# First dense layer as a seven-product scheme on pairs of token tiles, with w_out centred beforehand and the layer norm's factor moved to the output

## Chip, cores and metric

One core of one Trainium2 chip runs the whole program. The metric is the device time of a run in microseconds (us).

## What is computed

```python
x = attention(q, k, v)                     # 9 chunks of 64 positions, each for itself
P = exp(logits - max); 8 rounds of row and column scaling
out += P[:, e:e+1] * (relu(x @ w1[e]) @ w2[e])          # 8 experts
h = x @ w_in                               # 2304 x 512 by 512 x 1024: the first dense layer
solu = h * softmax(h)
ln = (solu - mean) / sqrt(var + 1e-6) * g_ln
return ln @ w_out                          # 1024 x 512: the second dense layer
```

w_in and w_out come as 64-bit floats.

## The kernel before

Every product runs on TensorE as three passes: an operand is split into a rounded part and a rest (`split`: ScalarE writes the rounded part, VectorE or GpSimd the rest), and hi\*hi, hi\*lo and lo\*hi are summed in PSUM.

The experts are worked off in 96 units `n` of 7 steps `i`. In step `i`, `l1` makes one of seven products (Winograd's form of Strassen's scheme, `PRODUCTS`: banks X, Y and Z, with VectorE's sums between them), and `l2s` makes a piece of the second expert product of an earlier pair of units; each is 6 matmuls of 384 columns. From unit 32 on both operands are loaded from DRAM through SP's queue (`w_load`, line 621), in the order in which the code issues them; an instruction that waits on a queue holds what is behind it. GpSimd makes `hT` and `ho_T` (`h_sums`, lines 681 and 673), the sums that `l2s` reads from its fourth operand on. `events` is a table of such work by step number. `second_sums` builds ten units' w2 operands on GpSimd and stores them (line 556).

`prep` is a queue of small steps that turn the 64-bit weights into split 32-bit ones (`mlp_steps`): from unit 35 on, one is taken in each of the steps 1, 3 and 5 of a unit. One tile of 128 x 512 takes seven VectorE instructions (lines 921 to 947), then `parts` (the split, GpSimd) and `store` (two DMAs, line 957).

The dense layers stand at the end. For each of 18 token tiles `t`: `mlp_x` loads x, `mlp_a` splits it, `mlp_b` makes h in two banks (24 matmuls of 512 columns, line 1005), the maximum (line 1019) and exp (line 1020); `mlp_n` makes solu (`un`, line 1025), its statistics (line 1030) and the normalised tile (line 1038); `mlp_c` transposes that (line 1050) and splits it; `mlp_d` makes the second product (24 matmuls, line 1062), and ScalarE and a DMA bring it out. The loop runs `mlp_b(s)`, `mlp_c(s - 1)`, `mlp_n(s)`, `mlp_d(s - 2)`. Before it stands the change-over: the 14 last pieces of `l2s` (k = 0 to 13), each in a bank of its own, with `mlp_b(0)` after k = 7.

Of the kernel before, what the change touches and what calls it, by code (L numbers as in the profile page):

```python
# [44 lines left out]
def chunk_attention_sinkhorn_moe_solu_kernel(  # L45
# [865 lines left out]

    def mlp_steps(n):
        i, j = divmod(n, 8)
        s = {}
        ts, stt = nc.vector.tensor_scalar, nc.vector.scalar_tensor_tensor


        def one():
            s["lo"], s["hi"] = raw64[n][:, :, 0], raw64[n][:, :, 1]
            s["b"] = two([P, 512], U32, f"wb{n}")  # L920
# [30 lines left out]
        def parts():  # L951
            s["p"] = [two([P, 512], F32R, f"wp{n}_{s_}") for s_ in range(2)]
            split(*s["p"], s["b"].bitcast(F32), nc.gpsimd)

        def store():
            for s_ in range(2):
                nc.sync.dma_start(
                    out=kept[i, s_][:, j * 512:(j + 1) * 512], in_=s["p"][s_].bitcast(F32)
                )

        return [one, two_, three, round_, rounded, size, flush_, parts, store]
# [3 lines left out]
    def load_in(kk, s_):  # L965
        t = six([P, F], F32R, f"mi{kk}_{s_}")
        nc.sync.dma_start(out=t.bitcast(F32), in_=kept[0, s_][:, kk * F:(kk + 1) * F])
        m_in[kk, s_] = t

    def load_out(n0, n1):  # L970
        for n in range(n0, n1):
            f, s_ = divmod(n, 2)
            if n % 3 == 0:
                m_out["t"] = six([P, 3, DM], F32R, f"mo{n}")
            t = m_out["t"]
            nc.sync.dma_start(
                out=t[:, n % 3].bitcast(F32), in_=kept[1, s_][:, f * DM:(f + 1) * DM]
            )
            m_out[f, s_] = t[:, n % 3]
# [14 lines left out]
    def mlp_a(t):  # L994
        x = xa.pop(t)
        xm[t] = [wtile([P, KD, P], F32R, f"xm{t}_{i}") for i in range(2)]
        split(xm[t][0], xm[t][1], x)

    def mlp_b(t):
        x = xm.pop(t)  # L1000
        ph = bank2(f"mh{t}")
        for n in range(2):
            for kk in range(KD):
                for i, (a, c) in enumerate(PASSES3):
                    nc.tensor.matmul(  # L1005
                        ph[:, n * 512:(n + 1) * 512],
                        x[a][:, kk, :],
                        m_in[kk, c][:, n * 512:(n + 1) * 512],
                        start=(kk == 0 and i == 0),
                        stop=(kk == KD - 1 and i == 2),  # L1010
                    )
# [3 lines left out]
        su = small.tile([P, 1], F32, tag="su", name=f"su{t}")  # L1015
        st = small.tile([P, 2, 6], F32, tag="st", name=f"st{t}")
        mv = small.tile([P, 2], F32, tag="mv", name=f"mv{t}")
        r2 = small.tile([P, 1], F32, tag="r2", name=f"r2{t}")
        nc.vector.tensor_reduce(out=nm, in_=ph, axis=AX.X, op=ALU.max, negate=True)  # L1019
        nc.scalar.activation(out=ex, in_=ph, func=AF.Exp, bias=nm, scale=1.0, accum_out=su)  # L1020
        stage[t] = (ph, ex, un, su, st, mv, r2)

    def mlp_n(t):
        ph, ex, un, su, st, mv, r2 = stage.pop(t)
        nc.vector.tensor_tensor(out=un, in0=ph, in1=ex, op=ALU.mult)  # L1025
# [3 lines left out]
        for i in range(2):  # L1029
# [26 lines left out]
    def mlp_d(t, f0=0, f1=KF):  # L1056
# [15 lines left out]
        nc.scalar.activation(out=ob, in_=po.pop(t), func=AF.Copy)  # L1072
# [3 lines left out]
    with tc.manual_schedule():  # L1076
# [103 lines left out]
        )  # L1180

# [5 lines left out]
        for n, u in enumerate(PLAIN):  # L1187
# [16 lines left out]
        for n in range(NM):  # L1204
# [30 lines left out]
            if n == NM - 1:  # L1235
                for t in range(3):
                    mlp_x(t)
            apart = n < 4
            parts = [(j, d, i) for d in (0, 2) for j in range(2) for i in range(2)]
            for i in range(7):  # L1240
# [9 lines left out]
                if n == NM - 1:  # L1250
                    load_in(*divmod(i, 2))
# [4 lines left out]
                if n > NU + 2 and i in (1, 3, 5) and prep:  # L1256
# [85 lines left out]
```

## Time and profile before

| | |
|---|---|
| median of 3 runs | 1758.02 us (1757.84 to 1758.71) |
| profiled execution | 1758.82 us, its span 1757.0 us |
| PE busy | 1736.6 us (99%), 10809 matmuls |
| DVE (VectorE) busy | 1371.0 us (78%) |
| POOL (GpSimd) busy | 1095.3 us (62%) |
| ACT (ScalarE) busy | 620.0 us (35%) |
| DMA, mean over the span | 274 GB/s |

Spans of time are counted from the first instruction. PE is TensorE's matmul row; busy shares are averages over stages with different limits.

### The profile page before, as it was taken

How to read it: one execution, taken by the hardware profiler on the slowest of the kernel's cores; microseconds unless marked ns; L12 is line 12 of the kernel's file. 1: busy time of each engine (PE TensorE's matmuls, PEld its weight loads, DVE VectorE, ACT ScalarE, POOL GpSimd, SP SyncE). 2: the span in 40 equal slices, each digit the busy share in tenths (PEclk: the TensorE clock that was granted, in tenths of full speed). 3: DMA queues.
4: the chain of work that ended last, by engine and by line, in shares of the span. 5: the costliest groups of instructions: out<-in, count | busy, mean ns of one | idle time of the engine just before them, and what ended most of it. 6: DMA issues, size and time to landing. Idle time of an engine off the chain costs nothing. (4 is left out here: it accounts for less than half of the span.)

```text
span 1757.0 us, 32067 instructions
## 1 busy us (share of the span) xinstructions
PE 1736.6 (99%) x10809; PEld 1683.5 (96%) x10809; DVE 1371.0 (78%) x2258; ACT 620.0 (35%) x1415; POOL 1095.3 (62%) x1203
## 2 busy tenths in 40 slices
PE   8999999999999999999999999999999999999999
PEld 7899999999999999999999999999999999988887
DVE  7878888888987777777777788878787877776664
ACT  6734444444444223333332222222323232223222
POOL 3867889888898277778777756665656565400000
PEclk9999999999999999999999999999999999999999
DMA  9867899899899999989989999888888887921210
GB/s 215 228 218 264 309 317 344 311 336 331 319 324 322 356 329 344 333 296 349 314 293 345 355 337 353 310 285 286 283 265 268 285 273 254 319 99 46 66 49 30
DMA packets 299203, 481.45 MB, mean 274 GB/s; under 512 B 47248, under 2 KB 99616, under 8 KB 299040
## 3 DMA queue, kind: packets, MB, share of 16 engines
q1 hardware_dynamic: 298320, 475.47, 79.2%
q10 hardware_dynamic: 720, 3.93, 0.5%
q8 instruction: 87, 1.43, 0.3%
q14 instruction: 76, 0.62, 0.1%
HBM read 332.94 MB, written 146.35 MB: 273 GB/s over the span
## 5 line engine op out<-in xcount | busy, mean ns | idle before, releaser
L673 POOL TENSOR_TENSOR ho_T<-hT,ho_T 128x384 fp32r<-128x384 f32 x252 | 275.8, 1096 | 195.0 <-ACT ho_T L672 174.7
L796 PE MATMUL y<-h,w_A 128*128 128x384 f32 x1536 | 303.7, 335 | 0.5 <-DVE acc L823 0.5
L796 PEld LDWEIGHTS y<-h,w_A 128*128 128x128 f32 x1536 | 269.1, 188 | 1.4 <-ACT w_S L599 1.1
L672 ACT ACTIVATE ho_B<-hp 128x384 fp32r<-128x384 f32 x192 | 101.0, 526 | 414.7 <-DVE hp L706 406.5
L847 PE MATMUL y<-ho_T,wl_S 128*128 128x384 f32 x1152 | 230.6, 335 | 1.5 <-DMA wl_S<-wk 1.5
L152 POOL TENSOR_TENSOR w_A<-raw,w_A 128x256 fp32r<-128x256 f32 x224 | 173.2, 786 | 82.1 <-ACT w_A L151 77.7
L867 DVE TENSOR_TENSOR acc<-y,acc 128x768 f32<-128x768 f32 (+1 forms) x217 | 199.9, 923 | 23.3 <-PE y L847 23.2
L751 DVE TENSOR_TENSOR t<-Y,s 128x384 f32<-128x384 f32 x192 | 106.2, 553 | 136.6 <-PE Y L653 94.0
L847 PEld LDWEIGHTS y<-ho_T,wl_S 128*128 128x128 f32 x1152 | 202.1, 188 | 3.0 <-issue 1.9
L681 POOL TENSOR_TENSOR hT<-hp,hp 128x384 f32<-128x384 f32 x126 | 133.7, 1083 | 96.5 <-DVE hp L706 86.7
L672 ACT ACTIVATE ho_T<-hT 128x384 fp32r<-128x384 f32 x256 | 131.7, 516 | 124.5 <-POOL hT L681 119.8
L653 PE MATMUL Y<-x_T,wl_S 128*128 128x384 f32 x768 | 154.0, 334 | 0.3 <-DVE t L751 0.3
L847 PE MATMUL y<-ho_B,wl_A 128*128 128x384 f32 x768 | 153.5, 334 | 0.5 <-DMA wl_A<-wk 0.5
L653 PE MATMUL X<-x_B,wl_A 128*128 128x384 f32 x768 | 153.7, 334 | 0.0
L673 DVE TENSOR_TENSOR ho_B<-hp,ho_B 128x384 fp32r<-128x384 f32 x192 | 143.6, 748 | 3.9 <-ACT ho_B L672 3.3
L681 POOL TENSOR_TENSOR hT<-hp,hT 128x384 f32<-128x384 f32 x126 | 144.9, 1150 | 0.0
L1036 POOL TENSOR_TENSOR r<-r,mhalf 128x1 f32<-128x1 f32 x18 | 9.9, 550 | 208.5 <-DVE r L1033 208.5
L847 PEld LDWEIGHTS y<-ho_B,wl_A 128*128 128x128 f32 x768 | 134.8, 188 | 1.0 <-DVE acc L867 0.8
L653 PEld LDWEIGHTS Y<-x_T,wl_S 128*128 128x128 f32 x768 | 134.8, 188 | 0.9 <-DVE t L751 0.9
L653 PEld LDWEIGHTS X<-x_B,wl_A 128*128 128x128 f32 x768 | 135.0, 188 | 0.0
L823 DVE TENSOR_TENSOR acc<-y,acc 128x768 f32<-128x768 f32 (+1 forms) x132 | 118.9, 901 | 5.3 <-PE y L796 4.7
L152 POOL TENSOR_TENSOR w_S<-ws,w_S 128x256 fp32r<-128x256 f32 x128 | 103.0, 822 | 7.8 <-ACT w_S L151 7.8
(169 smaller groups left out, 3453.5 us busy)
## 6 DMA issues: line engine op xcount, KB each, us to landing
wl_S<-wk SPq DMA_DIRECT2D x512, 256.0 KB, 4.9
wl_A<-wk SPq DMA_DIRECT2D x384, 256.0 KB, 4.9
wk<-w_S SPq DMA_DIRECT2D x256, 256.0 KB, 3.6
wk<-w_A SPq DMA_DIRECT2D x192, 256.0 KB, 3.4
raw<-in_moe_w_dram SPq DMA_DIRECT2D x71, 512.0 KB, 6.1
sh<-spread SPq DMA_DIRECT2D x64, 192.0 KB, 5.3
kept<-wp SPq DMA_DIRECT2D x32, 256.0 KB, 4.6
xk_T<-x_T SPq DMA_DIRECT2D x8, 768.0 KB, 4.3
```

What stands on the lines that cost most here:

```text
L152: (eng or nc.vector).tensor_tensor(out=lo, in0=src, in1=hi.bitcast(F32), op=ALU.subtract)
L653: nc.tensor.matmul(b, w[:, a, kk, :], x[:, c, kk, :], start=(first and kk == 0 and n == 0), stop=(kk == 1 and n == 2), skip_group_check=no ...
L672: nc.scalar.activation(out=hi, in_=x, func=AF.Copy)
L673: f = lambda: eng.tensor_tensor(out=lo, in0=x, in1=hi.bitcast(F32), op=ALU.subtract)
L681: eng.tensor_tensor(out=hb[m, n], in0=hb[m, a], in1=hb[m, b], op=ALU.subtract)
L751: nc.vector.tensor_tensor(out=c_of[n], in0=bank_, in1=c_of[other], op=ALU.add)
L796: nc.tensor.matmul(y, wo2[u, f"A{d // 2 + 1}{f + 1}"][:, a, i * P:(i + 1) * P], h[:, c, f, :], start=(f == 0 and n == 0), stop=(f == 1 and ...
L823: nc.vector.tensor_tensor(out=at, in0=y, in1=at, op=ALU.add)
L847: nc.tensor.matmul(y, wo2[unit(m + q_)[1], wn][:, a, i * P:(i + 1) * P], hop[m // 2, bn][:, q_, c, :], start=(q_ == 0 and o == 0), stop=(q ...
L867: nc.vector.tensor_tensor(out=at, in0=y, in1=at, op=ALU.add)
L1036: nc.gpsimd.tensor_tensor(out=r2, in0=r2, in1=mhalf, op=ALU.pow)
```

## The change

- `mlp_b` takes two tiles: A is 256 tokens x 512, B is w_in, each in 2 x 2 blocks. Seven products of 6 matmuls take the place of eight (48 matmuls). `mlp_s` makes the four sums of A's blocks and `mlp_a` splits them, both with GpSimd. B's four sums are made while w_in is converted (`less`), so `store` writes 28 pieces of 256 KB where it wrote 16, and `load_in` fetches them in the order of use. X and C12 lie in the pair's first double bank, C21 and C22 in its second; Y and Z have a single bank each.
- w_out's rows are scaled by g_ln and stored (`put_g`), then `mean_steps` loads them again, adds them up on GpSimd, takes the mean over the 1024 rows with one matmul (`wmean`), subtracts it from each piece, and splits and stores it. So the layer norm needs no mean taken off. Its factor is applied as ScalarE's scale when the output leaves PSUM; `mlp_n` loses two VectorE instructions and gains one of GpSimd.
- `prep` is taken in steps 0, 1 and 2, and in steps 0 to 5 once 64 or fewer are left. The w_in tiles go in the order B11, B12, B22, B21 of each half.
- `second_sums`' last three steps come 1, 3 and 5 steps later; the last pair's w2 loads come 4 steps sooner.
- The loop runs over 9 pairs; the change-over makes a whole pair after k = 7.

```diff
     def mlp_steps(n):
...
+        def store(n_=None):
             for s_ in range(2):
+                k = 4 * M_OPS.index(n_) + 2 * s_ + c
+                to = kept_in[:, k * 512:(k + 1) * 512]
+                nc.sync.dma_start(out=to, in_=s["p"][s_].bitcast(F32))
...
+        put = lambda v: [lambda: parts(v), lambda: store(v)]
+        if name == "B11":
+            return steps[:-1] + [lambda: (flush_(), keep_b())] + put("B11")
+        if name == "B12":
+            return steps[:-1] + [
+                lambda: (flush_(), keep_b()), lambda: less("T1", "B12", "B11")
+            ] + put("T1")
+        if name == "B22":
+            return steps + put("B22") + [
+                lambda: (less("T3", "B22", "B12"), less("T2", "B22", "T1"))
+            ] + put("T3") + put("T2")
+        return steps + put("B21") + [lambda: less("T4", "B21", "T2")] + put("T4")
+
+    def mean_steps():
...
+        r = [lambda: (load(0, vtile), load(1, two), nc.gpsimd.memset(ratio, 1.0 / F))]
+        for j in range(1, 8):
+            r.append(lambda j=j: (load(j + 1, two) if j < 7 else None, add(j)))
+        r += [lambda: None] * 3 + [lambda: (mean(), load(0, two))]
+        for j in range(8):
+            r.append(lambda j=j: (load(j + 1, two) if j < 7 else None, less(j)))
+            r.append(lambda j=j: parts(j))
+            r.append(lambda j=j: store(j))
+        return r
...
+    def mlp_s(r):
+
+        x0, x1 = xa[2 * r], xa[2 * r + 1]
+        ts = nc.gpsimd.tensor_tensor
...
+    def mlp_a(r):
...
+            split(*p, src, nc.gpsimd)
...
+    def mlp_b(r, i):
+
+        wn, xn, bn = PRODUCTS[i]
+        first = i in (0, 1, 4)
...
+        if i == 0:
+            mb["s1"] = two([P, 512], F32, f"ms{r}")
+            nc.scalar.activation(out=mb["s1"], in_=b, func=AF.Copy)
+        for to, x, other in {
+            1: (("t0", b, "s1"),), 3: (("t1", b, "s1"), (r1[:, 512:], mb.get("Z"), "t1")),
+            5: ((r1[:, :512], b, "s1"),), 6: ((r0[:, 512:], b, "t0"),),
+        }.get(i, ()):
...
+            nc.vector.tensor_tensor(out=to, in0=x, in1=mb[other], op=ALU.add)
+        if i == 5:
+            mlp_e(2 * r + 1, r1)
+        elif i == 6:
+            mlp_e(2 * r, r0)
...
-        nc.vector.tensor_tensor(out=r2, in0=r2, in1=su, op=ALU.mult)
-        nc.vector.tensor_scalar(
-            out=un, in0=un, scalar1=mv[:, 0:1], scalar2=r2, op0=ALU.subtract, op1=ALU.mult
-        )
-        ln[t] = un
+        nc.gpsimd.tensor_tensor(out=r2, in0=r2, in1=su, op=ALU.mult)
...
-        nc.scalar.activation(out=ob, in_=po.pop(t), func=AF.Copy)
+        nc.scalar.activation(out=ob, in_=po.pop(t), func=AF.Copy, scale=r2s.pop(t))
...
-                event(g + 7 + k, f[k])
+                event(g + 7 + k + (0, 1, 3, 5)[max(k - 6, 0)], f[k])
...
-                        event(7 * (m + 2) + 2 * n - 5,
+                        event(7 * (m + 2) + 2 * n - (9 if m == NM - 2 else 5),
...
-                if n > NU + 2 and i in (1, 3, 5) and prep:
+                if n > NU + 2 and (i < 3 or len(prep) <= fast and i != 6) and prep:
...
             if k == 7:
-                mlp_b(0)
-                mlp_a(2)
+                for i in M_ORDER:
+                    if i == 5:
+                        mlp_a(1)
+                    mlp_b(0, i)
+                mlp_m(1)
+                mlp_m(0)
...
+        for r in range(1, NR):
+            t1, t0 = 2 * r + 1, 2 * r
+            if r + 1 < NR:
+                mlp_s(r + 1)
+            for i in M_ORDER:
+                mlp_b(r, i)
+                if r == 1 and i == 3:
+                    mlp_n(1)
+                    mlp_n(0)
+            mlp_m(t1)
+            mlp_m(t0)
+            if r + 1 < NR:
+                mlp_a(r + 1)
+            mlp_d(t1 - 2)
+            mlp_c(t1)
+            mlp_n(t1)
+            for _ in range(2):
+                if sums:
+                    sums.popleft()()
...
+            mlp_n(t0)
+            mlp_d(t0 - 2)
+            mlp_c(t0)
```

`M_ORDER` is (0, 1, 4, 3, 2, 5, 6). Three places of the instruction order follow.

VectorE, in the loop of the dense layers. Before, one tile (`lnt`: the split's rest; `un`: solu; `xm`: x):

```order
L1019 TENSOR_REDUCE nm_20577<-mh_20550 128x1
L152 TENSOR_TENSOR lnt_0_1_20585<-lt_0_20588,lnt_0_0_20584 128x512
L152 TENSOR_TENSOR lnt_1_1_20587<-lt_1_20595,lnt_1_0_20586 128x512
L1025 TENSOR_TENSOR un_20576<-mh_20550,ex_20575 128x1024
L1026 TENSOR_SCALAR su_20578<-su_20578 128x1
L1027 RECIPROCAL su_20578<-su_20578 128x1
L1028 TENSOR_TENSOR r_20581<-su_20578 128x1
L1030 BN_STATS st_20579<-un_20576 128x6 x2
L1031 BN_AGGR mv_20580<-st_20579 128x2
L1033 TENSOR_SCALAR r_20581<-mv_20580,r_20581 128x1
L1037 TENSOR_TENSOR r_20581<-r_20581,su_20578 128x1
L1038 TENSOR_SCALAR un_20576<-un_20576,mv_20580,r_20581 128x1024
```

Now, from the second tile's split of one pair into the next pair (`mt`: t0 and t1; `mh`: the two double banks):

```order
L1198 TENSOR_SCALAR r_20428<-mv_20427,r_20428 128x1
L152 TENSOR_TENSOR lnt_0_1_20467<-lt_0_20470,lnt_0_0_20466 128x512
L152 TENSOR_TENSOR lnt_1_1_20469<-lt_1_20477,lnt_1_0_20468 128x512
L1164 TENSOR_TENSOR mt_20507<-mY_20500,ms_20498 128x512
L1164 TENSOR_TENSOR mt_20522<-mY_20500,ms_20498 128x512
L1164 TENSOR_TENSOR mh_1_20491<-mZ_20509,mt_20522 128x512
L1164 TENSOR_TENSOR mh_1_20491<-mY_20500,ms_20498 128x512
L1175 TENSOR_REDUCE nm_20540<-mh_1_20491 128x1
L1164 TENSOR_TENSOR mh_0_20490<-mZ_20509,mt_20507 128x512
L1175 TENSOR_REDUCE nm_20553<-mh_0_20490 128x1
L1181 TENSOR_TENSOR un_20539<-mh_1_20491,ex_20538 128x1024
L1181 TENSOR_TENSOR un_20552<-mh_0_20490,ex_20551 128x1024
```

The first sum of a pair (`mt`, t0) stands behind the statistics and both splits of the tile before it, and the statistics no longer stand ahead of the transposes of their own tile.

GpSimd, two units near the experts' end, before (`hT`, `ho_T`: the second expert product's sums and their splits):

```order
L681 TENSOR_TENSOR hT_18033<-hp_11_17959,hp_01_18003 128x384
L681 TENSOR_TENSOR hT_18035<-hp_01_18003,hp_00_17910 128x384
L673 TENSOR_TENSOR ho_T_18055<-hT_18033,ho_T_18055 128x384
L681 TENSOR_TENSOR hT_18058<-hp_11_17959,hT_18035 128x384
L673 TENSOR_TENSOR ho_T_18100<-hT_18035,ho_T_18100 128x384
L681 TENSOR_TENSOR hT_18103<-hp_10_17980,hT_18058 128x384
L673 TENSOR_TENSOR ho_T_18145<-hT_18058,ho_T_18145 128x384
L673 TENSOR_TENSOR ho_T_18197<-hT_18103,ho_T_18197 128x384
```

And now (`wg`: a scaled piece of w_out, `wp`: its split's rest):

```order
L681 TENSOR_TENSOR hT_18443<-hp_11_18360,hp_01_18409 128x384
L681 TENSOR_TENSOR hT_18445<-hp_01_18409,hp_00_18304 128x384
L673 TENSOR_TENSOR ho_T_18467<-hT_18443,ho_T_18467 128x384
L681 TENSOR_TENSOR hT_18470<-hp_11_18360,hT_18445 128x384
L1031 TENSOR_TENSOR wg_18387<-wg_18387,wmean 128x512
L152 TENSOR_TENSOR wp_1_18516<-wg_18387,wp_0_18515 128x512
L673 TENSOR_TENSOR ho_T_18519<-hT_18445,ho_T_18519 128x384
L681 TENSOR_TENSOR hT_18522<-hp_10_18383,hT_18470 128x384
L1031 TENSOR_TENSOR wg_18490<-wg_18490,wmean 128x512
L673 TENSOR_TENSOR ho_T_18569<-hT_18470,ho_T_18569 128x384
L152 TENSOR_TENSOR wp_1_18618<-wg_18490,wp_0_18617 128x512
L673 TENSOR_TENSOR ho_T_18621<-hT_18522,ho_T_18621 128x384
```

Four instructions of 512 columns now stand among the eight of 384 that `l2s` needs.

SP's queue in the last unit, before (`mi`: w_in's pieces, `wl_..._1`: w2 operands of the last pairs):

```order
L967 DMA mi_0_19018<-kept_0_133 128x1024
L621 DMA wl_A_1_19020<-wk_123 128x512
L621 DMA wl_A_1_19022<-wk_124 128x512
L967 DMA mi_1_19044<-kept_1_134 128x1024
L967 DMA mi_0_19067<-kept_0_133 128x1024
L621 DMA wl_A_1_19069<-wk_125 128x512
L621 DMA wl_A_1_19071<-wk_126 128x512
```

And now:

```order
L621 DMA wl_A_1_19087<-wk_125 128x512
L621 DMA wl_A_1_19089<-wk_126 128x512
L1063 DMA mi_19115<-kept_in 128x512
L1063 DMA mi_19117<-kept_in 128x512
L1063 DMA mi_19119<-kept_in 128x512
L1063 DMA mi_19130<-kept_in 128x1536
L621 DMA wl_A_1_19132<-wk_123 128x512
L621 DMA wl_A_1_19134<-wk_124 128x512
L621 DMA wl_A_1_19140<-wk_125 128x512
L621 DMA wl_A_1_19142<-wk_126 128x512
```

The last pair's first w2 operands (wk_125, wk_126) stand ahead of w_in's pieces instead of between them.

## Rows read from the trace of the kernel before

**Rows 1.** windows; stretch, length, busy us (instructions), clock, DMA share, GB/s

```profile
634.00:1100.00 466.00, 462.02 (x2653) 458.97 (x2652) 367.74 (x562) 139.58 (x301) 346.49 (x341) 1.00 0.94 330
...
1407.00:1506.00 99.00, 99.00 (x573) 99.00 (x572) 69.19 (x105) 27.24 (x57) 59.96 (x59) 1.00 0.82 263
...
1523.00:1559.00 36.00, 34.06 (x172) 29.23 (x171) 26.07 (x52) 7.52 (x15) 3.12 (x4) 1.00 0.65 233
...
1559.00:1754.00 195.00, 194.42 (x923) 161.87 (x921) 122.50 (x233) 53.99 (x98) 8.80 (x16) 1.00 0.15 49
```

**Rows 2.** chain that ended last, dense layers; start, us, what

```profile
1515.81 1.04 PE y L847 x6
...
1700.78 5.49 PE po L1062 x24
...
1706.26 5.44 PE mh L1005 x24
...
1711.71 0.88 PE lt L1050 x8
...
1753.46 0.60 ACT ob L1072
```

**Rows 3.** waits of PE, whole span; total us, times, longest us

```profile
PE Z L653 <- DVE X L751: 2.0, 3, 0.9
...
PE y L847 <- DMA wl_A<-wk: 1.7, 2, 1.2
...
PE y L847 <- DMA wl_S<-wk: 1.5, 2, 1.3
```

**Rows 4.** PE's timeline, change-over; start, us, instructions

```profile
1522.93 4.33 PE L847 MATMUL y<-ho_B,wl_A 128*128 128x384 f32 x24
...
1559.07 5.71 PE L1062 MATMUL po<-mo,lnt 128*128 128x512 f32 x24
```

**Rows 5.** instruction groups from 1560 on; busy us, mean ns, idle before

```profile
L152 DVE TENSOR_TENSOR lnt<-lt,lnt 128x512 fp32r<-128x512 f32 x34 | 21.9, 686 | 31.3 <-ACT lnt L151 31.3
...
L1030 DVE BATCH_NORM_STATS2 st<-un 128x6 f32<-128x512 f32 x32 | 20.5, 683 | 0.0
...
L1019 DVE TENSOR_REDUCE nm<-mh 128x1 f32<-128x1024 f32 x16 | 19.6, 1225 | 21.9 <-PE mh L1005 21.9
...
L1025 DVE TENSOR_TENSOR un<-mh,ex 128x1024 f32<-128x1024 f32 x16 | 19.4, 1215 | 0.0
...
L1020 ACT ACTIVATE ex<-mh,nm 128x1024 f32<-128x1024 f32 x16 | 17.9, 1117 | 92.0 <-DVE nm L1019 92.0
...
L1038 DVE TENSOR_SCALAR un<-un,mv,r 128x1024 f32<-128x1024 f32 x16 | 13.0, 813 | 0.6
...
L875 DVE TENSOR_TENSOR acc<-acc,acc 128x768 f32<-128x768 f32 x7 | 6.7, 953 | 0.0
...
L1033 DVE TENSOR_SCALAR r<-mv,r 128x1 f32<-128x1 f32 x16 | 3.4, 214 | 0.6
```

**Rows 6.** instruction groups of DVE, 634 to 1500

```profile
L751 DVE TENSOR_TENSOR t<-Y,s 128x384 f32<-128x384 f32 x118 | 65.3, 553 | 99.0 <-PE Y L653 59.6 <-POOL hT L681 12.9 <-POOL ho_T L673 10.9
...
L875 DVE TENSOR_TENSOR acc<-acc,acc 128x768 f32<-128x768 f32 x7 | 8.1, 1162 | 0.0
```

**Rows 7.** windows, 5 us of the change-over

```profile
1525.00:1530.00 5.00, 4.42 (x24) 3.78 (x24) 5.00 (x11) 1.52 (x3) 0.15 (x1) 1.00 1.06 386
```

**Rows 8.** DVE's timeline near 740

```profile
738.48 1.50 DVE L925 SCALAR_TENSOR_TENSOR wb<-wd,wb 128x512 uint32<-128x512 uint32 x1
```

**Rows 9.** PE's timeline near 741

```profile
741.37 1.33 PE L653 MATMUL Z<-x_B,wl_S 128*128 128x384 f32 x6 [0.72 <-DVE X L751]
```

**Rows 10.** waits of SP's queue, 634 to 1420

```profile
SPq L556 <- POOL w_S L602: 29.1, 19, 3.0
...
SPq L957 <- POOL wp L152: 13.5, 6, 4.3
```

**Rows 11.** instruction group of POOL, 634 to 1500

```profile
L152 POOL TENSOR_TENSOR wp<-wb,wp 128x512 fp32r<-128x512 f32 x16 | 20.9, 1305 | 17.1 <-ACT wp L151 17.0
```

More of the change, by code (lines that the diff above doesn't have):

```diff
@@ L949, in flush_, with put_g, parts @@
                 nc.scalar.activation(out=f, in_=f, func=AF.Copy, scale=g_sb[:, j:j + 1])
-        def parts():
+        def put_g():
+            nc.sync.dma_start(
+                out=kept_g[:, j * 512:(j + 1) * 512], in_=s["b"].bitcast(F32)
+            )
+        def parts(n_=None):
+            f = s["b"].bitcast(F32) if n_ in (None, name) else carried[n_]
             s["p"] = [two([P, 512], F32R, f"wp{n}_{s_}") for s_ in range(2)]
-            split(*s["p"], s["b"].bitcast(F32), nc.gpsimd)
@@ new lines, in mlp_steps, with keep_b @@
+        steps = [one, two_, three, round_, rounded, size, flush_]
+        if i == 1:
+            return steps + [put_g]
+        def keep_b():
+            carried[name] = s["b"].bitcast(F32)
+        put = lambda v: [lambda: parts(v), lambda: store(v)]
[5 more added lines that the diff above has]
+            ] + put("T1")
@@ new lines, in mlp_steps, with load, add, mean @@
+        if name == "B22":
[4 more added lines that the diff above has]
+    def mean_steps():
+        s = {}
+        def load(j, new):
+            s[j] = new([P, 512], F32, f"wg{j}")
+            nc.sync.dma_start(out=s[j], in_=kept_g[:, j * 512:(j + 1) * 512])
+        def add(j):
+            x = s.pop(j)
+            nc.gpsimd.tensor_tensor(out=s[0], in0=s[0], in1=x, op=ALU.add)
+        def mean():
+            pm = bank("wmean")
+            nc.tensor.matmul(pm, ratio, s.pop(0), start=True, stop=True)
+            s["m"] = vtile([P, 512], F32, "wmean")
+            nc.scalar.activation(out=s["m"], in_=pm, func=AF.Copy)
+        def less(j):
+            nc.gpsimd.tensor_tensor(out=s[j], in0=s[j], in1=s["m"], op=ALU.subtract)
+        def parts(j):
+            s["p", j] = [two([P, 512], F32R, f"wp{8 + j}_{s_}") for s_ in range(2)]
+            split(*s["p", j], s.pop(j), nc.gpsimd)
+        def store(j):
+            for s_, p in enumerate(s.pop(("p", j))):
@@ L957, in store @@
                 nc.sync.dma_start(
-                    out=kept[i, s_][:, j * 512:(j + 1) * 512], in_=s["p"][s_].bitcast(F32)
+                    out=kept_out[s_][:, j * 512:(j + 1) * 512], in_=p.bitcast(F32)
                 )
-        return [one, two_, three, round_, rounded, size, flush_, parts, store]
-    m_in, m_out = {}, {}
[L965 to L968, printed above, removed]
+        r = [lambda: (load(0, vtile), load(1, two), nc.gpsimd.memset(ratio, 1.0 / F))]
@@ new lines, in mean_steps, with load_in @@
+        for j in range(1, 8):
[6 more added lines that the diff above has]
+        return r
+    m_in, m_out = {}, {}
+    def load_in(n):
+        if n < 3:
+            t = vtile([P, 1, 512], F32R, f"mi{n}")
+            k0, k1 = n, n + 1
+        else:
+            t = six([P, 3, 512], F32R, f"mi{n}")
+            k0, k1 = 3 * n - 6, min(3 * n - 3, 28)
+        nc.sync.dma_start(
+            out=t[:, :k1 - k0].bitcast(F32).rearrange("p k x -> p (k x)"),
+            in_=kept_in[:, k0 * 512:k1 * 512],
+        )
+        for k in range(k0, k1):
+            x, r = divmod(k, 4)
+            m_in[M_OPS[x], r // 2, r % 2] = t[:, k - k0]
@@ L992, in mlp_x @@
         xa[t] = x
[L994 to L1010, printed above, removed]
-                    )
+    xsum = {}
@@ new lines, in chunk_attention_sinkhorn_moe_solu_kernel @@
+    mb = {}
+    def mlp_b(r, i):
+        wn, xn, bn = PRODUCTS[i]
+        first = i in (0, 1, 4)
+        if i == 0:
+            mb["r0"], mb["r1"] = bank2(f"mh{r}_0"), bank2(f"mh{r}_1")
+            mb["X"] = mb["r0"][:, :512]
+        elif first:
+            mb[bn] = bank(f"m{bn}{r}")
+        r0, r1, b = mb["r0"], mb["r1"], mb[bn]
+        x = xm.pop((r, wn))
+        for kk in range(2):
+            for n, (a, c) in enumerate(PASSES3):
+                nc.tensor.matmul(
+                    b, x[a][:, kk, :], m_in[xn, c, kk],
+                    start=(first and kk == 0 and n == 0),
+                    stop=(kk == 1 and n == 2),
+                    skip_group_check=not first,
+                )
+        if i == 0:
+            mb["s1"] = two([P, 512], F32, f"ms{r}")
[4 more added lines that the diff above has]
+        }.get(i, ()):
+            if isinstance(to, str):
+                mb[to] = two([P, 512], F32, f"m{to}{r}")
+                to = mb[to]
+            nc.vector.tensor_tensor(out=to, in0=x, in1=mb[other], op=ALU.add)
[3 more added lines that the diff above has]
+            mlp_e(2 * r, r0)
@@ L1235, in chunk_attention_sinkhorn_moe_solu_kernel @@
             if n == NM - 1:
+                assert not prep, len(prep)
                 for t in range(3):
+                    load_in(t)
+            if n == NM - 2:
+                for t in range(2):
                     mlp_x(t)
```

136 lines of the change are left out of this document (93 added, 43 removed).

## Prediction

> Times are of the profiled execution before (1758.82 us: a span of 1757.0 us and 1.82 us around it). Its median of three runs is 1758.02 us, 0.8 us less; the sum is made against the execution, and 0.8 us is taken off at the end.
>
> **What bounds the kernel now.** I first read the busy time by stretches [rows 1]. The reader is to see that TensorE is the bound nearly everywhere: 99.00 of 99 us near the experts' end, 194.42 of 195 us in the dense layers' loop, at a granted clock of 1.00. VectorE has 122.50 us of those 195. Only two stretches leave something: the 466 us in which weights are converted lose 4.0 us, and the change-over from 1523 to 1559 us loses 1.9 us of busy time.
>
> The chain that ended last comes next [rows 2]. In the loop it is TensorE alone, in a triple for each tile: 24 matmuls of the second layer (5.49 us), 24 of the first (5.44 us), eight transposes (0.88 us). So a matmul of 512 columns costs 5.44 / 24 = 0.227 us, and a pair of tiles 23.6 us. At the end ScalarE's copy starts at 1753.46, and some 3.5 us with its DMA end the span; the change leaves that tail as it is. Six matmuls of 384 columns take 1.04 us there, so an expert unit of 14 such groups takes 14.56 us.
>
> What TensorE waited for [rows 3]: 2.0 us for VectorE's sum in bank X, in three waits, and 3.2 us for w2 operands from DRAM, in four. The change-over read in order of time [rows 4] runs from 1522.93 to 1559.07, 36.1 us, for 14 x 1.04 + 3 x 5.44 + 2 x 0.88 = 32.6 us of work: 3.5 us lost.
>
> **The change part by part.**
>
> *Matmuls taken away.* 18 x 24 = 432 become 9 x 42 = 378. They lie on the path, in a stretch where nothing else ends last: 54 x 0.227 = **-12.2 us**. The mean of w_out adds one: +0.2 us.
>
> *VectorE in the loop.* Per pair it loses two normalisations of 0.813 us and two rests of x (which I take as long as lnt's rest, 0.686 us), and gains five sums of 512 columns, of which one operand is in PSUM [rows 5]. Such a sum is bounded by the 384-column one, 0.553 us [rows 6], and by lnt's rest, 0.686; I take the upper, since its shape and its operands are the same. That is +0.4 us per pair on some 14.8 us (63% of 23.6 us), in 22.2 us: VectorE isn't the bound, but its order may be. I count from the start of a pair's products, 1.36 us each. The sixth ends at 8.2; sum and maximum (1.225 us) twice bring it to 12.0, then exp (1.117 us) and two solu (1.215 us) to 14.4. TensorE asks for the first tile's transposes at 9.5 + 5.5 = 15.0, and that tile's solu is done near 13.1: covered. Behind it stand two rests, the statistics (two of 0.683 us and five of up to 0.214 us, 2.2 us), in the first four of the loop's pairs two sums of the last pass (0.953 us each), the second statistics and rests, and only then the next pair's t0. That lands near 26.4, and TensorE's fourth product, which overwrites Y, asks at 22.2 + 4.1 = 26.3. So four pair starts are about level, and I price each at 0.3 us with the handing over; pairs without those sums have 1.8 us in hand. If the cover went, each microsecond by which t0 is late would cost one per pair start. The four waits: +1.2 us.
>
> Those sums read both operands from SBUF: 1.162 us each while GpSimd is two thirds busy [rows 6], and 0.953 us in the loop, where it has 8.80 of 195 us [rows 1, 5]. GpSimd now makes four sums and the rests of x there, mostly before VectorE comes to the statistics, so I keep 0.953. The Trainium skill's SBUF — State Buffer, SBUF: two separate sides, says that VectorE with two SBUF inputs and GpSimd share a port pair that one of them holds for a whole instruction while the other blocks; by that rule each of these sums could wait out a full GpSimd instruction, and two in a pair would add up to 2.6 us at each of the four starts. The rows agree in direction only, with 0.2 us on average.
>
> *The first pair of the loop* has both statistics of the pair before between C22 and C21: 4.5 us, so the maximum and solu end near 16.4 where TensorE asks at 15.0. +1.5 us.
>
> *The change-over.* x's rests leave VectorE, whose queue made TensorE wait between the pieces of l2s. After the pair's products, piece 12 wants the bank of piece 8, whose sum now stands behind both solu: it is free near 14.4 - 9.5 = 4.9 us after the products, and wanted at 4 x 1.04 = 4.2. I take 1.2 us with the handing over. Ahead of it the DMAs: 28 pieces of 256 KB instead of 16, so 7.3 MB. At the 386 GB/s that the change-over reached [rows 7], all of them, and the w2 operands between them (ten and more pieces), are in about 30 us after their start near 1506.5, some 3 us before the seventh product wants the last. Covered; without that each microsecond late is one on the path, once. So the change-over loses 1.2 us and the pairs 1.5 + 1.2 us, 3.9 us against 3.5 us before: **+0.4 us**.
>
> *The conversion in the experts' stage.* All of it lies beside TensorE, so only waits count. The waits for bank X come from a conversion step that step 3 puts ahead of the sum: 1.50 us on VectorE at 738.48 [rows 8], and TensorE's matmul into Z, idle 0.72 us, at 741.37 [rows 9]. Steps 0 to 2 leave that place free: -2.0 us. The waits for w2 fall where SP, in order, stands at a store whose GpSimd half isn't done: 29.1 us in 19 waits for `second_sums`, 13.5 us in six for the split weights [rows 10]. The loads behind such a store come late. Moving the first back frees some (-1.2 us); but the split weights are now stored one step behind their split instead of two, 14 for w_in (two DMAs each) where there were eight: +1.0 us.
>
> *The mean.* Its stretch lies where TensorE now loses nothing and GpSimd has 59.96 of 99 us [rows 1], 8.8 us per unit. Seven sums in about 1.2 units, then 16 instructions in four units at 1.305 us, the price of a split's rest of that size [rows 11]: 9.1 + 10.6 = 19.7 us in 17, then 20.9 + 35.2 = 56.1 us in 58.2. GpSimd is full for five units and some 3 us late. What it makes is read about five steps (10 us) after its hp is there, so most is covered; VectorE's buffers and SP's stores wait with it. I bound the loss by 0 and 8 us and take 2.0, nearer to 0 because of those 10 us. The scaled pieces add 8 loads of w_out and 8 stores of 256 KB, small against the 330 GB/s of the 466 us stretch; nothing for them.
>
> Conversion and mean together: -2.0 - 1.2 + 1.0 + 2.0 = **-0.2 us**.
>
> **Sum:** -12.2 + 0.2 + 0.4 - 0.2 = -11.8 us: an execution of 1747.0 us, and 1746.2 us for the median.
>
> **Rivals.**
> 1. *The experts' stage gets rid of its waits.* All 5.2 us of rows 3 go and the mean costs nothing: 5 us better than the sum, 1741.2 us. For it: GpSimd's lateness is under the 10 us of cover. Against: SP waits for GpSimd more often.
> 2. *GpSimd becomes the bound in the mean's stretch.* If its instructions stretch as VectorE's did beside it (1.162 / 0.953 = 1.22), 75.8 us become 92 us in 75 us; less the 10 us of cover, 7 us of waits instead of 2, to which SP's held loads add: 1751 to 1755. It decides once GpSimd's demand passes some 85 us. Against: its rows were taken with VectorE busy already.
> 3. *The pairs become bound by their chain*, the other side. The place is t0, behind the second tile's statistics and rests in VectorE's queue. Each microsecond late there costs eight; from 1.5 us on nothing is left of the gain, and at 1.8 us the median is 1746.2 + 14.4 - 1.2 (priced above) = 1759.4. It needs the statistics or the rests to be late in all pairs, also in those with 1.8 us in hand. For it: 69% of VectorE's time in one queue. Against: nothing else in that queue waits for TensorE's last product. By the Trainium skill's SBUF — State Buffer, SBUF: two separate sides, at its worst, four of the eight starts would come 2.6 us later and the median would be 1756.6 us.
> 4. *The first layer's products are not the bound*, so that 54 matmuls fewer give nothing: only if some other engine ended last in the loop, which rows 2 deny. Below 1 in 50, inside rival 3's chance.
>
> **How the numbers follow.** My forecast has 0.64, rival 1 0.13, rival 2 0.16, rival 3 (with 4) 0.07. The predicted time is the forecast's. Within it the unknown prices reach from about 1743 (no mean cost, no pair starts late) to 1751 (6 us more of mean or starts). For 8 in 10 the range takes in most of rival 1 and two thirds of rival 2: 1739.5 to 1754. A measurement of this kernel tells 0.2% (3.5 us) from no change. Faster by more than that means below 1754.5: forecast, rival 1 and most of rival 2, 0.88. Within it: a rest of rival 2 and rival 3's near side, 0.07. Slower: 0.05.
>
> **What would show it.** In the loop the chain should be TensorE alone, with 42 matmuls into mh, mY and mZ in about 9.5 us and a pair in about 22.2 us; waits for VectorE's mt at four pair starts, and one of about 1.5 us for un in the first pair. In the experts' stage no wait of a matmul into Z for the sum in X. In the mean's stretch GpSimd busy over 95%, TensorE losing about 2 us. It is wrong if a pair takes 23 us or more, if TensorE waits in the change-over for mi, or if the stretch with the mean loses over 6 us.

## The result, and the profile after

The changed kernel is slower: 1766.81 us median (1766.09 to 1771.35, 4 runs) against 1758.09 us (1757.84 to 1758.71, 4 runs), a ratio of 1.0053 (95% interval 1.0042 to 1.0065). The forecast was 1746.2 us. The profiled execution has a span of 1765.1 us, 8.1 us more than before.

First the windows of the changed kernel, in three of the stretches of [rows 1], with the same columns:

```profile
634.00:1100.00 466.00, 452.80 (x2564) 447.72 (x2563) 345.16 (x532) 137.68 (x295) 347.65 (x341) 0.99 0.92 323
...
1407.00:1506.00 99.00, 99.00 (x570) 98.52 (x569) 71.64 (x106) 30.88 (x62) 87.94 (x79) 1.00 0.97 346
...
1559.00:1754.00 195.00, 191.32 (x923) 160.04 (x922) 141.51 (x253) 67.49 (x124) 69.51 (x94) 1.00 0.19 62
```

The loss is in the first row: TensorE is busy for 452.80 of 466 us, where it was 462.02, and 2564 matmuls are on record there where 2653 were. At 14.56 / 84 = 0.173 us each, the 89 that are missing would be 15.4 us: 9.2 us of it are idle time, the rest matmuls that took longer, as behind the two stalls shown below. In the second row, where w_out's mean is made, TensorE loses nothing; the third holds the end of the change-over, with three waits that come below. PE's timeline divides the 8.1 us: here is the start of the last 14 pieces of `l2s`, one pair of the loop, and the mean's matmul, in the changed kernel:

```profile
1431.21 1.02 PE L1026 MATMUL wmean<-wg,ratio 128*128 128x512 f32 x2
...
1539.19 4.33 PE L847 MATMUL y<-ho_B,wl_A 128*128 128x384 f32 x24
...
1661.38 1.62 PE L1148 MATMUL mh<-mi,xm_A 128*128 128x512 f32 x6
...
1671.00 5.61 PE L1223 MATMUL po<-mo,lnt 128*128 128x512 f32 x24
...
1683.61 1.62 PE L1148 MATMUL mh<-mi,xm_A 128*128 128x512 f32 x6
```

The pieces start at 1539.19 where they started at 1522.93 [rows 4]: **the experts' stage takes 16.3 us longer**. What is behind them takes 1765.1 - 1539.19 = 225.9 us where it took 234.1: **the dense layers gain 8.2 us**. A pair is 1683.61 - 1661.38 = 22.23 us, its products 9.62 us, near the 22.2 and 9.5 us forecast.

What TensorE waited for in the changed kernel, from 634 us on (total us, times, longest us), to be held against [rows 3]:

```profile
PE Y L653 <- DVE t L751: 6.5, 5, 4.1
PE y L847 <- DMA wl_S<-wk: 5.3, 3, 4.5
PE y L847 <- DVE acc L867: 3.5, 4, 1.4
...
PE lt L1211 <- DVE un L1181: 1.2, 1, 1.2
PE mY L1148 <- DVE mt L1164: 1.1, 1, 1.1
```

The waits for bank X are gone. In their place stand VectorE's t and w2 operands; the rows for acc, un and mt belong to the change-over and the dense layers. The two longest waits in PE's timeline, with what follows:

```profile
766.28 1.21 PE L847 MATMUL y<-ho_B,wl_S 128*128 128x384 f32 x6
771.62 1.41 PE L653 MATMUL Y<-x_T,wl_A 128*128 128x384 f32 x6 [4.13 <-DVE t L751]
772.83 2.12 PE L847 MATMUL y<-ho_B,wl_S 128*128 128x384 f32 x6
...
988.84 2.26 PE L847 MATMUL y<-ho_T,wl_S 128*128 128x384 f32 x6 [4.46 <-DMA wl_S<-wk]
990.89 2.12 PE L653 MATMUL X<-x_B,wl_A 128*128 128x384 f32 x6
```

Why is t late at 771? VectorE's timeline of the changed kernel:

```profile
762.83 0.54 DVE L706 SCALAR_TENSOR_TENSOR hp<-X,sh 128x384 f32<-128x384 f32 x1
771.01 0.56 DVE L751 TENSOR_TENSOR t<-Y,s 128x384 f32<-128x384 f32 x1 [7.64 <-POOL hT L681]
```

VectorE stands 7.64 us for GpSimd's `hT`, though t doesn't read it. t, s, hp, hT, wc, wp and the tiles of `second_sums` share one pool of 14 buffers (`two`), and t takes the buffer from which hT reads. GpSimd's timeline in the same stretch:

```profile
763.93 1.02 POOL L673 TENSOR_TENSOR ho_T<-hT,ho_T 128x384 fp32r<-128x384 f32 x1 [1.01 <-ACT ho_T L672]
764.90 1.02 POOL L681 TENSOR_TENSOR hT<-hp,hT 128x384 f32<-128x384 f32 x1
766.00 1.29 POOL L152 TENSOR_TENSOR wp<-wb,wp 128x512 fp32r<-128x512 f32 x1
767.25 0.72 POOL L602 TENSOR_TENSOR w_S<-w2s_S,w_S 128x256 fp32r<-128x256 f32 x1
768.91 0.99 POOL L673 TENSOR_TENSOR ho_T<-hT,ho_T 128x384 fp32r<-128x384 f32 x1 [0.94 <-ACT ho_T L672]
769.98 0.99 POOL L681 TENSOR_TENSOR hT<-hp,hT 128x384 f32<-128x384 f32 x1
```

And ScalarE's, which makes the other halves of the splits:

```profile
762.95 0.42 ACT L599 ACTIVATE w_S<-w2s_S 128x256 fp32r<-128x256 f32 x1 [3.88 <-POOL hT L681]
...
768.01 0.42 ACT L599 ACTIVATE w_S<-w2s_S 128x256 fp32r<-128x256 f32 x1 [2.40 <-POOL w_S L602]
768.33 0.51 ACT L672 ACTIVATE ho_T<-hT 128x384 fp32r<-128x384 f32 x1
```

GpSimd isn't short of time: it takes turns with ScalarE. The split of prep's tile (`wp`) stands right ahead of a split of `second_sums` (`w_S`), and hT behind both. ScalarE's next `w_S` waits for the one before (2.40 us), and the half of `ho_T` that GpSimd needs stands behind it.

The other wait is for a transfer. SP's queue from 634 to 1407 us, before:

```profile
SPq L440 <- DVE hp L706: 1.7, 6, 0.3
```

and in the changed kernel:

```profile
SPq L440 <- DVE hp L706: 26.3, 13, 3.3
```

Line 440 is `load_share`, which fetches the experts' share tiles `sh`, two at a time, into the pool `V` of six. A line of the change that the prediction passed over puts converted blocks there:

```diff
-            s["b"] = two([P, 512], U32, f"wb{n}")
+            new = vtile if name in ("B11", "B12") else two
+            s["b"] = new([P, 512], U32, f"wb{n}")
```

B11 stays from its first conversion step until T4 is made, some 45 steps at three a unit. With two of the six taken, `sh` for the next unit must wait until hp has read the one before, and the w2 loads stand behind it in the queue. 26.0 of the 26.3 us lie between 834 and 1034 us, where the share loads come 10 to 35 us apart in both kernels; ahead of that they come 40 us and more apart. That B11 and B12 are what takes the room is read from the code and these rows: no run puts them elsewhere.

The change-over, in PE's timeline of the changed kernel:

```profile
1544.28 1.32 PE L847 MATMUL y<-ho_B,wl_S 128*128 128x384 f32 x6 [0.76 <-DVE acc L867]
1546.57 1.33 PE L847 MATMUL y<-ho_B,wl_S 128*128 128x384 f32 x6 [0.97 <-DVE acc L867]
1548.31 2.01 PE L847 MATMUL y<-ho_T,wl_S 128*128 128x384 f32 x10 [0.41 <-DVE acc L867]
...
1565.81 2.35 PE L847 MATMUL y<-ho_T,wl_A 128*128 128x384 f32 x12 [1.39 <-DVE acc L867]
1586.13 1.07 PE L1211 MATMUL lt<-ident,un 128*128 128x128 f32 x8 [1.22 <-DVE un L1181]
1598.71 1.66 PE L1148 MATMUL mY<-mi,xm_S 128*128 128x512 f32 x6 [1.07 <-DVE mt L1164]
```

The first waits have their cause in these rows of VectorE's timeline:

```profile
1540.62 3.13 DVE L681 TENSOR_TENSOR hT<-hp,hp 128x384 f32<-128x384 f32 x2
...
1544.68 1.37 DVE L681 TENSOR_TENSOR hT<-hp,hT 128x384 f32<-128x384 f32 x1
```

beside these rows of GpSimd's, two splits of x and then two of hT that come after them:

```profile
1540.50 2.85 POOL L152 TENSOR_TENSOR xm_S<-xs,xm_S 128x512 fp32r<-128x512 f32 x2
...
1544.31 2.60 POOL L673 TENSOR_TENSOR ho_T<-hT,ho_T 128x384 fp32r<-128x384 f32 x2
```

In VectorE's timeline before, with GpSimd idle there, the same two hT took a third of that:

```profile
1526.22 1.01 DVE L681 TENSOR_TENSOR hT<-hp,hp 128x384 f32<-128x384 f32 x2
```

### The profile page after: what moved, and what is told of

Same layout as the page of the kernel before. It is cut to its first block, busy times and chain, and to the rows that moved or that the text cites. A ratio compares the mean times of both kernels' runs of the same rounds, so it can differ in the third digit from the quotient of the medians.

```text
span 1765.1 us, 32273 instructions
## 1 busy us (share of the span) xinstructions
PE 1731.2 (98%) x10757; PEld 1677.2 (95%) x10757; DVE 1375.1 (78%) x2249; ACT 639.0 (36%) x1449; POOL 1214.1 (69%) x1323
## 5 line engine op out<-in xcount | busy, mean ns | idle before, releaser
L673 DVE TENSOR_TENSOR ho_B<-hp,ho_B 128x384 fp32r<-128x384 f32 x192 | 149.1, 776 | 4.8 <-ACT ho_B L672 3.5
L706 DVE SCALAR_TENSOR_TENSOR hp<-X,sh 128x384 f32<-128x384 f32 x128 | 71.1, 555 | 46.1 <-PE X L653 22.6
```

Source lines behind the costliest of these rows:

```text
L673: f = lambda: eng.tensor_tensor(out=lo, in0=x, in1=hi.bitcast(F32), op=ALU.subtract)
L706: nc.vector.scalar_tensor_tensor(out=hp, in0=c, scalar=0.0, in1=share[visit[m], j], op0=ALU.max, op1=ALU.mult)
```

## The experiments

Three theories for the experts' stage: P, the place of prep's steps; V, the share tiles that lost two buffers; D, the later stores of `second_sums`. Each edit starts from the changed kernel. The pool V can't grow by two buffers, so V is tried by order: the load is issued where it needn't wait. The kernel before, run beside each, took 1757.3 to 1758.1 us in the median, so a difference under 1 us tells nothing.

**Prep in steps 1, 3 and 5 (e1).**

```diff
-                if n > NU + 2 and (i < 3 or len(prep) <= fast and i != 6) and prep:
+                if n > NU + 2 and (i in (1, 3, 5) or len(prep) <= fast and i != 6) and prep:
```

> Edit: prep's steps go back to 1, 3 and 5 of a unit (all but step 6 once 64 or fewer are left); all else as in the changed kernel. The changed kernel's experts' stage ends 16.3 us later than before's (last unit over at 1539.19 us instead of 1522.93). Theory P (placement): steps 0 to 2 put prep's split on GpSimd between the splits of second_sums, ScalarE and GpSimd wait for each other in turn and VectorE's t comes 4.13 us late at 771.62; then this kernel gets most of the 16.3 us back: 1752 to 1757 us. Theory V (share tiles): the blocks B11 and B12 hold two of the six V buffers that the experts' share tiles sh had to themselves, so SP's queue stands at the load of sh (26.3 us in 13 waits, none before) and the w2 loads behind come late; the place of prep's steps has no part in that: within 4 us of 1766.8. Theory D (delay): the stores of second_sums, 1, 3 and 5 steps later, hold buffers longer: also within 4 us of 1766.8.

1755.25 us (1753.65 to 1757.07, ratio to before 0.9986, 0.9977 to 0.9996): 11.6 us come back, as P has it. SP's wait at line 440 is still 21.6 us, yet both long waits of TensorE are gone: 1.01 us for t at 768.52 and 1.23 us for w2 at 978.45 are left.

**`second_sums` as before (e2).**

```diff
-                event(g + 7 + k + (0, 1, 3, 5)[max(k - 6, 0)], f[k])
+                event(g + 7 + k, f[k])
```

> Edit: the last three steps of second_sums go back to their steps (no 1, 3, 5 later). Theory D: the stores that come 3 and 5 steps later hold buffers that hT and t want, which makes the 4.13 us wait at 771.62: 1755 to 1761 us. Theories P and V: the wait for GpSimd's w_S in SP's queue comes back (29.1 us in 19 waits before, 15.4 in 8 now) on top of their own: 1766 to 1770 us.

1766.41 us (1765.24 to 1767.51; 1.0049, 1.0034 to 1.0064), and the 4.1 us wait stands. D falls: SP's waits for w_S at line 556 are 31.2 us again, as P and V have it, but the later stores neither cost nor bring any time that shows.

**`load_share` at step 4 (e3).**

```diff
-            if n >= NQ and v + 1 < len(visits) and n == max(visits[v][2], visits[v + 1][2] - 2):
+            share_due = (
+                n >= NQ and v + 1 < len(visits) and n == max(visits[v][2], visits[v + 1][2] - 2)
+            )
+            if share_due and n <= NU + 2:
                 load_share(v + 1)
...
+                if share_due and n > NU + 2 and i == 4:
+                    load_share(v + 1)
```

> Edit: from unit 35 on, load_share is issued at step 4 of its unit, not ahead of the unit's w1 loads, so that SP's queue no longer stands there while those loads could go; buffers as in the changed kernel. Theory V: the 26.3 us of SP's waits for hp at line 440 fall below 8 us, TensorE's waits for wl (6.2 us) go below 2 us, and with the clock that the 4.46 us stall at 988.84 cost, the time is 1756 to 1761 us; the 4.13 us wait for t at 771.62 stays. Theories P and D: SP's stand is a result of VectorE's lateness, not its cause; within 3 us of 1766.8.

1759.36 us (1758.55 to 1760.56; 1.0012, 1.0002 to 1.0021): 7.4 us come back. SP's queue in that kernel:

```profile
SPq L440 <- DVE hp L706: 1.2, 3, 0.9
```

TensorE's waits for w2 operands fell to 4.5 us, not below 2: those between 1064 and 1123 us are left, after the change of pass, where the kernel before waits too (1.15 us at 1111.95). The 4.13 us for t stay. So V is true of the w2 wait, and P of both waits: with prep moved (e1), SP's stand at line 440 no longer reached TensorE. That is why the two gains overlap.

**The three edits together (e4).**

> Edit: the edits of e1, e2 and e3 together. If those three places are all that the experts' stage lost, the stage ends within 3 us of before's 1522.93 plus 0.7 us, and the time is 1749 to 1753 us (1757.0 + 16.3 - 8.1 - 16.3, and 2 us around it). If the buffers that the conversion holds longer are a cause by themselves (theory H: wb of B22 and B21 in the pool of 14, split weights stored behind each split), over half of the 16.3 us stays: 1758 us or more.

1752.6 us (1751.24 to 1753.78; 0.997, 0.9958 to 0.9981), the stage over at 1524.54. The gains of the single edits, 11.6, 0.4 and 7.4 us, overlap: 14.2 us. Theory H as written, that over half of the loss stays while the blocks are held longer, falls. What buffers do was tried apart, further down.

What is it about steps 0 to 2? Two kernels move prep again, with `load_share` at step 4:

```diff
-                if n > NU + 2 and (i < 3 or len(prep) <= fast and i != 6) and prep:
+                if n > NU + 2 and (i in (0, 2, 4) or len(prep) <= fast and i != 6) and prep:
```

and the same with (3, 4, 5).

> Edit: load_share at step 4 (as in the run before that moved only that, 1759.4 us) and prep in the steps 0, 2 and 4 instead of 0, 1 and 2. Theory B (bunching): three conversion steps on end, 1.0 to 1.5 us each on VectorE and a split that GpSimd and ScalarE take turns in, leave no room to catch up; spread over every other step, whichever these are, the time is that of steps 1, 3 and 5, 1751 to 1754.5 us, and the wait for t at 771.62 (4.13 us) is under 1 us. Theory F (phase): only steps 1, 3 and 5 fall between the splits of second_sums and the sums into the banks; then 0, 2 and 4 stay at 1757 us or more.

> Edit: load_share at step 4, and prep in the steps 3, 4 and 5, on end but at the unit's other half. Theory B: as bad as 0, 1 and 2: 1757 to 1761 us, with single waits of TensorE for VectorE of over 2 us between 650 and 1050. Theory F: other phase, other outcome: 1755 or less.

Steps 0, 2 and 4: 1751.49 us (1750.28 to 1752.47; 0.9964, 0.9951 to 0.9977). Steps 3, 4 and 5: 1753.89 us (1753.19 to 1755.86; 0.9977, 0.9968 to 0.9987), with one wait of 4.0 us for a w2 operand. With 0, 2 and 4 the wait at 771.62 is gone, as B has it, and 0.85 and 1.21 us for t are left elsewhere; 3, 4 and 5 came out as F has it. On end, at that place, the steps cost 2.4 us more, not the 7.9 of steps 0 to 2, so neither theory holds as it stood. What is left is that P's steps collide with other work. Moving the other party tests that:

```diff
-                event(g + 7 + k + (0, 1, 3, 5)[max(k - 6, 0)], f[k])
+                event(g + 10 + k + (0, 1, 3, 5)[max(k - 6, 0)], f[k])
```

> Edit: the changed kernel with all ten steps of second_sums three steps later (loads as they are). Theory M (meeting): what costs is that wp's split of B22 and three splits of second_sums stand in one stretch of GpSimd's and ScalarE's queues (764.98 to 774 us); apart from each other the 4.13 us wait goes, and the time is 1757 to 1763 us unless another pair meets. Theory N: prep in steps 0 to 2 is late by itself wherever second_sums stands: a wait of over 3 us for t stays near 770, within 3 us of 1766.8.

1763.99 us (1761.62 to 1765.88; 1.0033, 1.0021 to 1.0044). The wait near 770 is gone, as M has it, with prep still in steps 0 to 2, so N falls. But TensorE waits 2.37 us for t at 856.31, where it waited 0.60, and VectorE stands 5.29 us for hT there: `w_S` and `ho_T` take turns, with no split of prep on GpSimd between 841.04 us and that wait. The w2 wait stays (3.45 us at 986.21; 4.46 in the changed kernel). The time lies just above M's range.

**One more buffer** is the test of what the collision costs through:

```diff
-        return work.tile(shape, dt, tag="two", bufs=14, name=name)
+        return work.tile(shape, dt, tag="two", bufs=15, name=name)
```

> Edit: the changed kernel with 15 instead of 14 buffers in the pool that t, s, hp, hT, wc, wp and second_sums' tiles share (room from three small tables); order of work as in the changed kernel. Theory H (buffers): in the changed kernel VectorE's t at 771.01 has stood 7.64 us for GpSimd's hT, which it doesn't read: it takes the buffer that hT's operand leaves, and GpSimd gets to hT only after four turns with ScalarE (wp, then three w_S). One more buffer lets t go ahead: TensorE's 6.5 us of waits for t fall below 2.5 us and the time is 1757 to 1762 us. Theory E (engines): the work itself is late, not the room: waits for t stay over 5 us, within 3 us of 1766.8.

1757.9 us (1756.28 to 1759.45; 1.0, 0.9991 to 1.001): 8.9 us come back with the order of work as it was, as H has it. TensorE waits 0.9 us for t in all, and VectorE at the spot has another releaser and little over half the wait:

```profile
767.67 0.56 DVE L751 TENSOR_TENSOR t<-Y,s 128x384 f32<-128x384 f32 x1 [4.29 <-POOL ho_T L673]
```

(Ahead of the hT that t stood for, GpSimd's rows show three turns with ScalarE, `wp`, one `w_S` and `ho_T`, not the four expected.) SP's wait at line 440 is still 24.2 us there, and the w2 wait 3.46 us. Taking these away too, by the place of the load, with prep in steps 0 to 2:

> Edit: the changed kernel with 15 buffers in the one pool and load_share at step 4, prep still in steps 0, 1 and 2, second_sums and the dense layers as in the changed kernel. Each alone gave 7 to 9 us (1757.9 and 1759.4 us). Theory R (room): lack of buffers in the two pools is the whole of what the experts' stage lost, and where prep's steps stand matters only through it: 1750 to 1753 us, as with the three edits of order (1752.6 us). Theory B (bunching): three conversion steps on end cost by themselves, with room for all: 1754.5 us or more.

1751.94 us (1750.59 to 1755.09; 0.997, 0.9957 to 0.9982), the stage over at 1524.00. SP waits for hp at line 440 no more, and theory R's time came: **one more buffer in the pool `two`, and a share load that needn't wait for its buffer, give back 15.2 of the 16.3 us, with prep where the change put it.** Spreading the steps alone gives back nearly as much: the stage of e1 ends at 1524.76 in its profiled execution, the fastest of ten. So the loss needs both, the lack of room and the place of the steps. The pool V itself got no room, so of V only the load's place is shown. No run gave the kernel before the extra buffer; its trace has 0.3 us of waits for t and 1.7 us of SP's for hp at line 440, so little was to be had there.

**The change-over.** The first pair's sums and splits come three and four steps earlier, which takes GpSimd's `xm` away from VectorE's hT:

```diff
-                    if i == 3:
+                    if i == 0:
                         mlp_s(0)
-                    if i == 5:
+                    if i == 1:
                         mlp_a(0)
```

> Edit: the changed kernel with the first pair's mlp_s and mlp_a in steps 0 and 1 of the last unit instead of 3 and 5, and nothing else. In the changed kernel VectorE's two hT at 1540.62 take 3.13 us and the one at 1544.68 1.37 us, while GpSimd splits xm (1539.05 to 1544.35); before, with GpSimd idle, two take 1.01 us and one 0.54. Theory L (the two engines hold each other up when both read SBUF): with the splits gone from there, hT take some 0.5 us each again and the three waits for acc at the start of the change-over (2.1 us together) fall below 0.7 us. Theory Q (VectorE's queue is simply longer there): hT stay at over 1 us on average and the waits stay over 1.5 us. The time is 1764 to 1767 us by either.

1765.59 us in one execution. The three waits (2.14 us) are gone, and the later hT take what they took before:

```profile
1541.82 1.52 DVE L681 TENSOR_TENSOR hT<-hp,hp 128x384 f32<-128x384 f32 x2
...
1544.20 0.54 DVE L681 TENSOR_TENSOR hT<-hp,hT 128x384 f32<-128x384 f32 x1
```

Theory L holds: the first two hT, 1.52 us instead of 1.01, stand beside GpSimd's last two `ho_T`, which end at 1542.46. All edits of the dense layers, with those of the experts' stage:

```diff
-                mlp_m(1)
-                mlp_m(0)
+            if k == 10:
+                mlp_m(1)
+            if k == 12:
+                mlp_m(0)
...
-                if r == 1 and i == 3:
-                    mlp_n(1)
-                    mlp_n(0)
+                if r == 1 and i in (1, 3):
+                    mlp_n(1 if i == 1 else 0)
```

> Edit: load_share at step 4, prep in 1, 3 and 5, and in the dense layers: the first pair's sums and splits (mlp_s, mlp_a) in steps 0 and 1 of the last unit instead of 3 and 5; its two solu after the pieces k = 10 and k = 12 instead of ahead of k = 8; the first pair's two statistics apart, after the second and the fourth product of the next pair. In the changed kernel TensorE loses 3.5 us in the change-over in four waits for acc (0.76, 0.97, 0.41, 1.39), 1.22 us for the first pair's solu and 1.07 us for mt. If these are what the edits aim at (GpSimd's splits beside VectorE's hT, solu ahead of the sums, both statistics ahead of C22), 4 us or more of those 5.8 go: 1747 to 1749.5 us against 1752.6 us of the kernel with the experts' part alone. If they only move, 1751.5 us or more.

1747.55 us (1746.52 to 1750.27; 0.9947, 0.993 to 0.9964), 5.1 us below the experts' part alone (e4, which also has `second_sums` as before, worth nothing that shows in e2). Of the six waits 0.40 us for mt is left.

**A version faster than the kernel before and the changed one.** Prep in 0, 2 and 4 with all of this, then with 15 buffers:

> Edit: load_share at step 4, prep in 0, 2 and 4, and the four edits of the dense layers of the run that had prep in 1, 3 and 5 (1747.55 us). Both parts add up if they are apart: 1751.5 less 5.0 us, 1745.5 to 1748 us.

> Edit: the kernel of the run beside it (load_share, prep in 0, 2, 4, dense layers) with 15 buffers. Theory H: the 2.1 us of waits for t that are left with prep in 0, 2, 4 go, 2 to 3 us below that kernel. Theory E: the same time within 1 us.

1746.88 us (1745.08 to 1748.32; 0.9936, 0.9921 to 0.9951) and **1745.08 us** (1744.7 to 1745.75; 0.9927, 0.9912 to 0.9942). The last is 1.8 us below its neighbour, between the theories, and their intervals overlap, so the times don't decide; the waits for t (2.0 us in the neighbour) are gone. What TensorE waits for in it, from 634 us on, all rows:

```profile
PE y L847 <- DMA wl_S<-wk: 2.1, 2, 1.4
PE y L847 <- DMA wl_A<-wk: 1.2, 1, 1.2
PE mZ L1152 <- DMA mi<-kept_in: 0.8, 1, 0.8
PE mY L1152 <- DVE mt L1168: 0.4, 1, 0.4
```

## Why the prediction was wrong

*Matmuls taken away, -12.2 us: right.* Nine pairs at 22.23 us instead of 23.58 make -12.2 us.

*The mean's matmul, +0.2 us: too low.* Its operands are not split, and it is recorded as two instructions, 1.02 us together; the unit with it takes 15.42 us instead of 14.56, +0.9 us.

*The mean's stretch, +2.0 us, and rival 2: not borne out.* GpSimd went to 87.94 of 99 us, not over 95%, and TensorE lost nothing but that matmul.

*VectorE in the loop: sizes right, one place wrong.* A sum of 512 columns took 0.69 us as taken. Pair starts were put at 0.3 us in four places, +1.2 us; one of them waits (1.07 us). The first pair was put at +1.5 us and waits 1.22 us. Rival 3 did not come about: from the loop's third pair on there is no wait.

*The change-over, 1.2 us: mis-sized.* From 1539.19 to the next pair's first product at 1569.66 there are 30.47 us for 14 x 1.04 + 7 x 1.36 + 2 x 0.88 = 25.84 us of work: 4.6 us lost. The bank of piece 8 cost 1.39 us, as seen; what was missed are the three waits ahead of it. The prediction counted x's rests off VectorE as a relief and didn't ask what GpSimd does to hT from its new place. It weighed the Trainium skill's rule (SBUF — State Buffer, SBUF: two separate sides) only for the loop's sums. There it wasn't put to the test: they took 0.95 us each as taken, but GpSimd's splits had ended at 1635.61 us in a pair whose sums start at 1637.22. In the change-over the trace agrees with it: VectorE's two hT, with two SBUF operands each, end at 1543.75, 0.4 us after GpSimd's two splits. All dense terms together: 4.6 + 1.4 + 1.35 (the two pairs over 22.23 us) = 7.4 us lost instead of 3.9 forecast and 3.5 before.

*The conversion in the experts' stage, -2.0 - 1.2 + 1.0 us: this step failed.* The waits for X did go, but the step priced work and queue order alone. It never asked which buffers the moved work holds. Measured, the stage is 16.3 us longer, 0.9 of it the mean's matmul: +15.4 us where -2.2 stood. The sum is then -12.2 + 3.9 (7.4 less the 3.5 of before) + 0.9 + 15.4 = 8.0 us, against 8.1 us between the spans. Runs show the cause: with one more buffer and the share load moved, 15.2 us come back (that kernel's stage ends at 1524.00). The -1.2 us for `second_sums` isn't seen either: with its steps put back (e2) SP stands 31.2 us at the stores instead of 15.4, and the time is the same. That VectorE's buffers wait when GpSimd is late stands in the prediction, but only for the mean's stretch, where nothing came of it. "Steps 0 to 2 leave that place free" was read from VectorE's queue; GpSimd's and ScalarE's queues, in which `wp` and `w_S` meet, weren't followed. And the rival on the other side was put into the loop, where the change saves work, not where it makes tiles live longer.

About 1 us of the stage (1524.00 against 1522.93) is left with both pools eased, as much as the mean's matmul costs; a single trace can't tell such a difference from chance. That kernel takes 1751.94 us, 5.7 above the forecast of 1746.2, as the dense terms and the waits that the conversion was to save are still off. The 1745.08 us of the last kernel don't bear the forecast out: some 5 us of it come from edits of the dense layers that the prediction didn't have.

## What to carry to other kernels

Where a change makes a tile live longer or puts it into another pool, list who else takes buffers there, and ask what an allocation waits for when the pool is full: the wait can show on an engine that reads nothing of what it waits for, and on a DMA queue it holds all that is behind it. Here a buffer more and a spread-out order cured the same lack, so their gains didn't add up. When work goes to GpSimd, look for VectorE instructions with two SBUF operands beside it.

## What the runs showed of the hardware

The two long stalls cost more than their length, as the granted clock falls behind them. Windows of the changed kernel (clock in the third column from the end):

```profile
770.00:775.00 5.00, 3.38 (x13) 3.38 (x14) 3.58 (x7) 1.54 (x4) 3.35 (x4) 0.77 0.72 233
...
990.00:995.00 5.00, 5.00 (x18) 5.00 (x17) 0.12 (x1) 0.91 (x2) 1.14 (x2) 0.54 1.00 326
```

After the 4.46 us of idleness TensorE is fully busy from 990 to 995 us with 18 matmuls in place of some 30, at a granted clock of 0.54, near the lower level (1.2 GHz of 2.4). The unit of the 4.13 us wait took 20.6 us (756.92 to 777.52), 6.0 more than 14.56. Behind the wait of 1.24 us at 1073.40 the clock was 1.00 (window of 1075 to 1080 us).

A 512-column matmul of unsplit f32 operands took 1.02 us, in two records of 0.59 us that overlap, where one of split operands takes 0.227.
